# A Fourier layer and eight routed experts on one core: four transform chunks change their neighbours, and the experts' row and weight loads change their place in the load queue

## The chip, the core and the metric

The kernel runs on one core of a Trainium2 chip. The core has a matrix engine (TensorE, PE in the profile, with its weight loads shown apart as PEld), three engines for elementwise work (VectorE is DVE, ScalarE is ACT, GpSimd is POOL) and SyncE (SP), which here does nothing but issue DMAs. Each engine runs its own instructions in order and waits on semaphores for the others. The metric is the device time of one execution in microseconds (us); smaller is better.

## The reference, cut to what matters

```python
# x is (8, 2496, 256); all arrays are float32
X = np.fft.rfft(x, axis=1)
Yr = Xr @ w_r - Xi @ w_i + b_r          # 256 x 256, the same for every frequency
Yi = Xr @ w_i + Xi @ w_r + b_i
Yr, Yi = shrink(Yr, 0.01), shrink(Yi, 0.01)   # sign(v) * max(|v| - 0.01, 0)
y = np.fft.irfft(Yr + 1j * Yi, n=2496, axis=1)

t = y.reshape(19968, 256)
logits = t @ w_gate + modality_bias[modality_id]      # 8 experts
e = argmax(logits); gate = softmax(logits)[e]
out = gate * (relu(t @ w1[e]) @ w2[e])                # 256 -> 1024 -> 256
```

## The kernel before

The transform over 2496 points is split as 39 times 64, and float32 operands are split into a high and a low part of which three products are summed. The work of one batch row (called a batch here, `b` = 0 to 7) goes through four steps on TensorE, and two batches are always in work:

- **Chunks** (`s1_chunk`, lines 298 to 320): the first transform, over 39 points. A batch has 11 chunks, each three matmuls of 117 rows by 512 columns (L311, L312, L313) into one PSUM bank, which ACT copies out (L316). Every second chunk SP writes 480 KB to a scratch in DRAM (L320). Each chunk needs its input split first (`s1_split`: a cast at L293 and a subtraction at L295).
- **Mixing stage** (ten pairs `p`): the second transform (L372), the products with the weights (L391, L403) and the shrinking (L408, L409). The loads of it come back from the scratch (`a_load`, L360).
- **64-row transform** (`is2_group`, five groups `g`): the first step back. Its matmuls (L431) use 64 of TensorE's 128 rows each and run in pairs, one on the upper 64 rows and one on the lower. DVE and ACT copy the two banks of a group out (L435).
- **Transposing products** (22 steps `j`): `pivot` (L445) gives 128-row products that ACT casts (L450) and DVE subtracts (L451); `is1` (L457 to L459) does the last transform on them three products at a time. Between them stand two pairs of the next batch's mixing stage (`s2`, at the start and after j = 15).

The order on PE, ACT, DVE and POOL is written out by hand in `build`; SP's order is set by the framework's scheduler. The chunks of batch b + 2 are dealt out over batch b. For b = 1 to 5, five of the eleven stand in the mixing stage (c = 0 to 4), four in the 64-row transform behind its groups 0 to 3 (c = 5 to 8), two among the transposing products (c = 9 and 10, at j = 8 and 11). For batch 0, four stand in the 64-row transform and seven among the transposing products. For batches 6 and 7 there are none left.

Lines 1551 to 1555 are the place in the 64-row transform:

```python
for g in range(5):
    at.is2_group(b, g)
    ...
    if b + 2 < nb and g < 4:
        at.s1_chunk(*s1.pop(0), inverse=True)
        at.s1_split(b + 2, 7 + g if b else 4 + g)
```

Behind the eighth batch come the **experts** (`Experts.run`). Rows were scattered by expert to DRAM (`xs`), and 40 units `i` go over them: 38 of 512 rows and two of 256. A unit has two halves (`grp` 0 and 1); in each, the first layer's products of one half (L1048) and the second layer's of another (L1119) take turns on PE. Unit i + 2's rows come by `load_x` (four DMAs L915, and L917), and its weights in four parts by `load_w(i + 2, n)` (n = 0 and 1: L882 or L883 and L884; n = 2 and 3: L877), on SP's queue. From the ninth unit on a weight part is only fetched when the expert changes. `prep(i + 2)` transposes the rows on DVE (L934) in the second half of unit i. Five of the units also carry a small remainder tile (`tiny`), whose raw weights are loaded by `load_raw` (L893, L897). Before, the rows of unit i + 2 and weight part 0 are asked for at the start of unit i, parts 1 and 2 in its middle, part 3 at its end.

Of the kernel before, what the change touches and what calls it, by code (L numbers as in the profile page):

```python
# [45 lines left out]
EARLY = (6 * SEQ - 8 * (TP - 1)) // TP + 1 - E  # L46
# [771 lines left out]
class Experts:  # L818
# [438 lines left out]
    def run(self, late, *tail):  # L1257

        nc = self.nc
        U = NP + NS  # L1260
        self.tags = {NPL - 1: [2, 4, 5, 6]}
        for i in range(NPL - 2, -1, -1):
            t = self.tags[i + 1]
            self.tags[i] = [t[3]] + [j for j in range(7) if j not in t]
        pieces = self.weight_sums()
        for i in range(2):
            self.load_x(i)
        self.rt.grid2 = self.rt.load_grid(self.cp, "c_grid2", 5 * E + 3)
        for n in range(4):
            self.load_w(1, n)  # L1270
            if n == 0:
                next(pieces)
        self.fold = self.cp.tile([128, TINY], F32, name="fold")
        with self.tc.issue_after(tail[0].ins), self.tc.issue_after(tail[1].ins):
            for _ in chain(self.prep(0), self.sums(0), self.parts(0)):
                pass
        nc.vector.reduce_sum(self.fold, self.ident.rearrange("p (g t) -> p t g", t=TINY), AX.X)
        self.fill(5)
        for _ in self.layer1(0, 0):
            pass  # L1280
        for _ in self.prep(1):
            pass
        every = (U - 8) // SLOTS
        for i in range(U):
            if i + 2 < U:
                assert i + 2 < EARLY or self.rt.late
                if i == NPL - 2:
                    assert next(pieces, None) is None
                self.load_x(i + 2)
                self.load_w(i + 2, 0)  # L1290
            k, at = divmod(U - 2 - i, every)
            k = U + SLOTS - 1 - k
            small = U <= k < U + SLOTS
            if small and at == 2:
                self.load_x(k)
                self.stage = self.load_raw(k)
            if small and at == 1:
                self.sort_half(k)
            if small and at == 0:
                self.side = self.tiny(k)  # L1300
            for grp in range(2):
                one = self.layer1(i + grp, 1 - grp) if i + grp < U else iter(())
                n1 = (8 if i + grp < NPL else 7 if i + grp < NP else 4) if i + grp < U else 0
                n2 = 2 * self.subs(i)
                two = self.layer2(i, grp)
                fill = {"o": iter(()), "x": self.parts(i + 1) if grp == 0 and i + 1 < U else iter(()),
                        "t": self.sums(i + 1) if grp == 0 and i + 1 < U else iter(()),
                        "p": self.prep(i + 2) if grp == 1 and i + 2 < U else iter(())}
                if self.rest:
                    fill["o"], self.rest = self.last(*self.rest), None  # L1310
                fills = self.FILL[grp] if grp or i >= NPL else self.FILL2 if i == NPL - 1 else self.FILL1
                for n, c in enumerate(self.order(n1, n2)):
                    next(one if c == "1" else two)
                    for f in fills.get(n, ""):
                        next(fill[f], None)
                    if n in self.LATE:
                        next(late, None)
                    if i < NPL - 2:
                        next(pieces, None)
                    if c == "2":  # L1320
                        next(self.stage, None)
                        if n % 3 == 0:
                            next(self.side, None)
                for g in (one, two, fill["o"], fill["t"], fill["x"], fill["p"]):
                    for _ in g:
                        pass
                if i + 2 < U:
                    if grp == 0:
                        self.load_w(i + 2, 1)
                    self.load_w(i + 2, 2 + grp)  # L1330
        for _ in self.side:
            pass
        self.finish(*self.rest)

        k = U + SLOTS
        more = nc.values_load(self.rt.ti[k:k + 1, 3:4], min_val=0, max_val=1,
                              skip_runtime_bounds_check_because="a flag")
        with self.tc.If(more > 0):  # L1338
            for i in range(k, k + MORE):
                self.load_x(i)  # L1340
                for _ in self.load_raw(i):
                    pass
                self.sort_half(i)
                self.half(i)
# [37 lines left out]
def build(tc, I, out, nb):  # L1382
    nc = tc.nc
    with ExitStack() as outer:
# [3 lines left out]
        with ExitStack() as ctx:  # L1388
            at = Attn(tc, I, nb)
# [15 lines left out]
            def s2(i, split=None):  # L1405
                if i < last:
                    low.append(at.s2_pair(*divmod(i, 10), ld.pop(i)))
                    xs[i] = next(low[-1])
                if split:
                    at.s1_split(*split)  # L1410

            def s2_low():
                for g in low:
                    next(g)
                low.clear()
# [48 lines left out]
            s1 = [(1, c) for c in range(11)]  # L1464
            for b in range(nb):
                done = b == nb - 1
                for p in range(10):
                    i = 10 * b + p
# [43 lines left out]
                    if b and p == 5 and b + 2 < nb:  # L1512
                        s1 = [(b + 2, c) for c in range(11)]
# [30 lines left out]
                if b == 0:  # L1544
                    at.s1_load(2, 5)
                    s1 = [(2, c) for c in range(11)]
                for g in range(5):
                    at.is2_group(b, g)
                    if done:
                        rt.scatter(2, at.mark)  # L1550
                    if not done and g in (1, 3):
                        sw.step()
                    if b + 2 < nb and g < 4:
                        at.s1_chunk(*s1.pop(0), inverse=True)
                        at.s1_split(b + 2, 7 + g if b else 4 + g)
                s2(10 * b + 10)
                more = 8
# [2 lines left out]
                for j in range(J):  # L1560
                    pend.append((j, at.pivot(b, j)))
                    if (j + 1) * left // J != j * left // J:
                        rt.scatter(1, at.mark)
                    if j == 15:
                        s2(10 * b + 11)
                    if len(pend) > 2:
                        jj, r = pend.pop(0)
                        at.is1(b, jj, *r, nc.scalar.copy if done or jj % 2 else nc.vector.tensor_copy)
                    if j in (2, 17):
                        s2_low()  # L1570
                    if not done and j in ((14, 19) if b else (9, 14, 19)):
                        sw.step()
                    if j == 6:
                        rt.bias(b)
                    if j % 3 == 2 and (j > 6 or b == 0) and s1:
                        at.s1_chunk(*s1.pop(0), inverse=True)
                    if b == 0 and j % 3 == 2 and more < 11:
                        at.s1_split(2, more)
                        more += 1
                    next(routing, None)  # L1580
# [62 lines left out]
```

## Time and profile before

| what | us |
|---|---|
| median of 3 runs | 1467.63 (1466.71 to 1468.15) |
| the profiled execution's own time | 1459.45 |
| its span, from first to last instruction | 1457.7 |
| PE busy in the span | 1415.0 (97%) |
| PEld busy in the span | 1354.5 (93%) |
| DVE, ACT, POOL busy in the span | 892.4, 779.9, 791.7 (61%, 54%, 54%) |

The profile is of one execution. A group row gives the busy time of like instructions and the idle time of the engine before them; a window row gives every engine's busy time in a stretch, with the number of its instructions, the granted clock of TensorE (1.00 is 2.4 GHz, 0.50 is 1.2 GHz) and the share of the DMA engines' time. In a timeline a row is one instruction, or several alike, with its start, its duration, and in brackets the idle time before it and what ended that. A matmul's duration is longer than the distance to the next one, since they are pipelined: what a matmul costs is the distance between starts.

### The profile page before, as it was taken

To read this page: it belongs to the slowest core of one execution; us is meant where nothing else is said; L and a number is where in the kernel's file an instruction comes from. 1 tells how busy PE (TensorE), PEld (TensorE's weight loads), DVE (VectorE), ACT (ScalarE), POOL (GpSimd) and SP (SyncE) were. 2 spreads that over 40 slices of the span, in tenths; PEclk is the share of its full clock that TensorE was granted. 3 is DMA by queue.
4 is the path that set the end of the run, shared out by engine and by line. 5 is a ranking of instruction groups with operands and counts; after the bars stand their busy time and mean duration, and the time that the engine had idled before them with its cause. 6 is when DMAs were issued, how large, how long until landed. Compare 5 with 4: busy or idle time off the path is not lost. (4 is left out here: it accounts for less than half of the span.)

```text
span 1457.7 us, 33928 instructions
## 1 busy us (share of the span) xinstructions
PE 1415.0 (97%) x12122; PEld 1354.5 (93%) x12122; DVE 892.4 (61%) x1729; ACT 779.9 (54%) x1690; POOL 791.7 (54%) x905
## 2 busy tenths in 40 slices
PE   8999999999999998999999999999999999999996
PEld 7898989898989888999999999899999999999995
DVE  6666666565666675667764565566656656666651
ACT  5566565555555352644435555455555555555542
POOL 2547676766677565366657644344444444454442
PEclk9999999999999999999999999999999999999999
DMA  8779686968686658488779369214212962592192
GB/s 299 212 216 293 205 289 209 291 203 278 191 293 188 213 160 283 158 235 267 224 280 280 87 223 319 55 40 111 59 43 54 291 196 46 170 308 60 38 335 106
DMA packets 242240, 284.54 MB, mean 195 GB/s; under 512 B 120761, under 2 KB 173865, under 8 KB 238995
## 3 DMA queue, kind: packets, MB, share of 16 engines
q1 hardware_dynamic: 222769, 240.22, 53.8%
q0 software_dynamic: 19168, 42.04, 9.0%
q8 instruction: 98, 1.61, 0.5%
q14 instruction: 75, 0.61, 0.1%
q10 hardware_dynamic: 130, 0.06, 0.0%
HBM read 320.24 MB, written 114.86 MB: 298 GB/s over the span
## 5 line engine op out<-in xcount | busy, mean ns | idle before, releaser
L1119 PE MATMUL y<-w,hh 128*128 128x256 f32 x2496 | 455.9, 277 | 0.0
L1119 PEld LDWEIGHTS y<-w,hh 128*128 128x128 f32 x2496 | 377.7, 189 | 3.7 <-issue 3.7
L1119 PE MATMUL y<-w,hl 128*128 128x256 f32 x1248 | 346.1, 277 | 1.5 <-DVE hl L1054 1.4
L1048 PE MATMUL X<-xh,w 128*128 128x256 f32 x1248 | 265.6, 278 | 2.0 <-issue 2.0
L1152 POOL DMA_INDIRECT out<-o,ix x156 | 155.5, 997 | 174.1 <-ACT o L1136 139.6
L1119 PEld LDWEIGHTS y<-w,hl 128*128 128x128 f32 x1248 | 235.1, 188 | 2.3 <-DVE hl L1054 2.1
L1048 PEld LDWEIGHTS X<-xh,w 128*128 128x128 f32 x1248 | 212.1, 189 | 4.1 <-issue 2.2
L1048 PE MATMUL X<-xl,w 128*128 128x256 f32 x624 | 173.2, 278 | 0.6 <-POOL xl L983 0.6
L1054 DVE SCALAR_TENSOR_TENSOR hl<-Y,hh 128x512 fp32r<-128x512 f32 x140 | 96.8, 691 | 99.3 <-ACT hh L1053 80.2
L1053 ACT ACTIVATE hh<-Y 128x512 fp32r<-128x512 f32 x140 | 83.8, 599 | 113.5 <-DVE Y L1057 93.6
L983 POOL TENSOR_TENSOR xl<-tr,xh 128x256 fp32r<-128x256 f32 x94 | 70.6, 751 | 119.4 <-ACT xh L982 118.4
L1048 PE MATMUL Z<-xh,w 128*128 128x256 f32 x608 | 128.8, 277 | 3.2 <-DVE Y L1057 3.2
L983 POOL TENSOR_TENSOR xl<-xt,xh 128x256 fp32r<-128x256 f32 x122 | 88.7, 746 | 67.2 <-ACT xh L982 67.0
L403 PE MATMUL mx<-wmix,Xh 128*128 128x256 f32 x640 | 116.1, 304 | 7.6 <-DVE mx L393 3.4
L619 POOL DMA_INDIRECT xs<-x1b,si x88 | 90.1, 1024 | 53.6 <-DVE pl L451 22.2
L1048 PEld LDWEIGHTS X<-xl,w 128*128 128x128 f32 x624 | 117.8, 189 | 1.1 <-POOL xl L983 0.8
L1062 ACT COPY v<-X 128x512 f32<-128x512 f32 x180 | 105.6, 587 | 16.5 <-PE X L1048 11.6
L619 POOL DMA_INDIRECT xs<-x,si x88 | 88.8, 1009 | 40.6 <-issue 19.6
L445 PE MATMUL pv<-pv,z 128*120 128x136 f32 x704 | 108.8, 280 | 1.7 <-DVE pl L451 0.8
L1048 PEld LDWEIGHTS Z<-xh,w 128*128 128x128 f32 x608 | 102.8, 188 | 3.6 <-DVE Y L1057 3.6
L403 PEld LDWEIGHTS mx<-wmix,Xh 128*128 128x128 f32 x640 | 92.4, 190 | 14.8 <-issue 5.8
L451 DVE TENSOR_TENSOR pl<-pv,ph 120x264 fp32r<-120x264 f32 x176 | 74.7, 430 | 50.9 <-ACT ph L450 33.3
(265 smaller groups left out, 3437.3 us busy)
## 6 DMA issues: line engine op xcount, KB each, us to landing
w<-wsp SPq DMA_DIRECT2D x96, 1024.0 KB
w<-wss SPq DMA_DIRECT2D x64, 1024.0 KB
w<-wsp SPq DMA_DIRECT2D x64, 768.0 KB
xt<-xs SPq DMA_DIRECT2D x152, 128.0 KB
x<-in_x SPq DMA_DIRECT2D x35, 512.0 KB
a<-scr SPq DMA_DIRECT2D x140, 128.0 KB
scr<-ev SPq DMA_DIRECT2D x35, 480.0 KB
wsp<-wh SPq DMA_DIRECT2D x64, 256.0 KB
```

Source lines behind the costliest of these rows:

```text
L403: nc.tensor.matmul(mx[:, i, :], t[:, c, 1 - i, :], self.w[:, i, c, lo, :], start=False, stop=n == 5, skip_group_check=True)
L445: nc.tensor.matmul(ps[:PK, c * 128:c * 128 + D // 2 + E], self.z[:, o:o + 3, :, :].rearrange("p n k r -> p (n k r)"), self.pv[:, c, :], st ...
L451: self.mark = nc.vector.tensor_sub(pl, ps[:PK, :GC], ph)
L619: i = self.nc.gpsimd.indirect_dma_start(out=self.xs, out_offset=bass.IndirectOffsetOnAxis(ap=si[:, k:k + 1], axis=0), in_=rows, in_offset= ...
L983: (nc.gpsimd if i or j in (0, 1, 6) else nc.vector).tensor_sub(sq(xl), v, sq(xh))
L1048: nc.tensor.matmul(ps[:, u, :], w1[:, lo, u, blk, :], x, start=start and u == k == 0, stop=k == 2, skip_group_check=True)
L1053: nc.scalar.activation(hh[:, par::2, o], v, AF.Relu)
L1054: nc.vector.scalar_tensor_tensor(hl[:, par::2, o], v, 0.0, hh[:, par::2, o], ALU.max, ALU.subtract)
L1062: nc.scalar.copy(v, ps)
L1119: nc.tensor.matmul(ps, h[:, q, o], w2[:, lo, q, :], start=grp == s % 2 == q == k == 0, stop=grp == 1 and q == 3 and k == 2, skip_group_che ...
L1152: ins = self.nc.gpsimd.indirect_dma_start(out=self.out, out_offset=bass.IndirectOffsetOnAxis(ap=ix, axis=0), in_=o, in_offset=None, bounds ...
```

## The change

Three things change, and no instruction is added or taken away.

For batches 1 to 5 no chunk stands in the 64-row transform any more. The four go among the transposing products, where the chunks now stand at j = 5, 8, 11, 14, 17 and 20. The input of the last one is split behind j = 5 instead of behind group 3. Batch 0 stays as it was.

In the experts, rows are asked for half a unit sooner, in the middle of unit i for unit i + 3, where the rows are complete by then. Weight part 2 moves from the middle of the unit to slot 7 of its second half.

```diff
@@ Experts.run
             if i + 2 < U:
-                assert i + 2 < EARLY or self.rt.late
                 if i == NPL - 2:
                     assert next(pieces, None) is None
-                self.load_x(i + 2)
+                if i + 2 not in self.xt:
+                    assert i + 2 < EARLY or self.rt.late
+                    self.load_x(i + 2)
                 self.load_w(i + 2, 0)
...
+                    if grp and n == 7 and i + 2 < U:
+                        self.load_w(i + 2, 2)
...
+                if grp == 0 and i + 3 < U and (i + 3 < EARLY or self.rt.late):
+                    self.load_x(i + 3)
                 if i + 2 < U:
-                    if grp == 0:
-                        self.load_w(i + 2, 1)
-                    self.load_w(i + 2, 2 + grp)
+                    self.load_w(i + 2, 3 if grp else 1)
@@ build, 64-row transform
-                    if b + 2 < nb and g < 4:
+                    if b == 0 and g < 4:
                         at.s1_chunk(*s1.pop(0), inverse=True)
+                    if b + 2 < nb and g < 4 and (g < 3 or b == 0):
                         at.s1_split(b + 2, 7 + g if b else 4 + g)
@@ build, transposing products
-                    if j % 3 == 2 and (j > 6 or b == 0) and s1:
+                    if j % 3 == 2 and (j > 3 or b == 0) and s1:
                         at.s1_chunk(*s1.pop(0), inverse=True)
+                        if b and j == 5:
+                            at.s1_split(b + 2, 10)
```

On PE, between groups 0 and 1 of batch 1's 64-row transform (`zs_0`, `zs_1` are the groups' banks, `s_3_5` is chunk 5 of batch 3):

```order
 L431 MATMUL zs_0_z<-c_q,x_67 128x128
 L431 MATMUL zs_0_x<-c_q,x_67 128x128
-L311 MATMUL s_3_5_1825<-x1h_5_1732,c_f 120x512
-L312 MATMUL s_3_5_1825<-x1h_5_1732,c_f 120x512
-L313 MATMUL s_3_5_1825<-x1l_5_1733,c_f 120x512
 L431 MATMUL zs_1_z<-c_q,x_67 128x128
 L431 MATMUL zs_1_x<-c_q,x_67 128x128
```

The chunk is gone from there, and group 1 follows group 0; the same holds behind groups 1 to 3, and in batches 2 to 5.

On PE, among batch 1's transposing products, where that chunk now stands (`pv_5` and `pv_6` are steps 5 and 6, `i_1_3` is the last transform of step 3):

```order
L445 MATMUL pv_5_2001<-pv,z_1804 120x136 x2
L457 MATMUL i_1_3_2011<-ph_3_1977,c_g 117x264
L458 MATMUL i_1_3_2011<-ph_3_1977,c_g 117x264
L459 MATMUL i_1_3_2011<-pl_3_1978,c_g 117x264
L311 MATMUL s_3_5_2016<-x1h_5_1732,c_f 120x512
L312 MATMUL s_3_5_2016<-x1h_5_1732,c_f 120x512
L313 MATMUL s_3_5_2016<-x1l_5_1733,c_f 120x512
L445 MATMUL pv_6_2026<-pv,z_1804 120x136 x2
```

Before, step 6 followed directly on the last transform of step 3.

On SP, behind the first loads of a remainder tile's raw weights (`x_67<-in_moe_w`), where `w_0_7707` is weight part 1, `w_0_7703` and `w_0_7704` are parts 2 and 3, and `xt` and `g` are unit 15's rows; before:

```order
L897 DMA x_67<-in_moe_w 128x2x256
...
L883 DMA w_0_7707<-wsp 128x4x384
...
L884 DMA w_0_7707<-wss 128x4x512
...
L877 DMA w_0_7703<-wsp 128x2048
...
L877 DMA w_0_7704<-wsp 128x2048
...
L915 DMA xt_12668<-xs 32x16x64
...
L917 DMA g_12669<-xs 128x4x2
```

and now:

```order
L897 DMA x_67<-in_moe_w 128x2x256
...
L915 DMA xt_12538<-xs 32x16x64
...
L917 DMA g_12539<-xs 128x4x2
...
L883 DMA w_0_7707<-wsp 128x4x384
...
L884 DMA w_0_7707<-wss 128x4x512
...
L877 DMA w_0_7703<-wsp 128x2048
...
L877 DMA w_0_7704<-wsp 128x2048
```

The rows' loads stood behind the three remaining weight parts and stand ahead of them now.

## Rows read from the trace of the kernel before

**Rows 1.** The page, busy time of each engine over the span:

```profile
PE 1415.0 (97%) x12122; PEld 1354.5 (93%) x12122; DVE 892.4 (61%) x1729; ACT 779.9 (54%) x1690; POOL 791.7 (54%) x905
```

**Rows 2.** Windows, the 64-row transform of batches 1 to 7, one row each:

```profile
core 0: us, PE busy (x) PEld busy (x) DVE busy (x) ACT busy (x) POOL busy (x), PEclk, DMA share, GB/s
...
133.15:147.42 14.27, 14.12 (x173) 11.55 (x172) 4.06 (x6) 7.55 (x13) 10.29 (x11) 1.00 0.72 220
206.49:220.35 13.86, 13.64 (x173) 11.18 (x172) 4.07 (x6) 7.66 (x13) 10.91 (x11) 1.00 0.65 194
277.65:292.75 15.10, 14.31 (x173) 11.62 (x172) 4.15 (x6) 7.43 (x13) 12.03 (x13) 1.00 0.74 238
350.33:368.24 17.91, 15.93 (x174) 12.98 (x173) 4.07 (x6) 7.70 (x13) 11.63 (x12) 0.90 0.63 196
426.76:441.45 14.69, 14.45 (x173) 11.67 (x172) 4.15 (x6) 7.36 (x13) 12.39 (x13) 1.00 0.71 223
499.85:509.88 10.03, 10.03 (x161) 9.91 (x160) 4.00 (x10) 3.33 (x5) 6.69 (x7) 0.90 0.49 165
567.37:583.90 16.53, 13.37 (x162) 11.76 (x161) 4.65 (x7) 4.16 (x7) 9.19 (x10) 0.90 0.91 249
```

**Rows 3.** Timeline of PE (start us, duration us, line, operands), batch 2's 64-row transform:

```profile
214.61 0.49 PE L311 MATMUL s<-x1h,c_f 117*120 117x512 f32 x1
...
215.50 0.37 PE L431 MATMUL zs_z<-c_q,x1b 64*128 64x128 f32 x1
...
215.72 0.27 PE L431 MATMUL zs_z<-c_q,x1b 64*128 64x128 f32 x1
...
217.28 0.27 PE L431 MATMUL zs_z<-c_q,x1b 64*128 64x128 f32 x1
...
217.49 0.49 PE L311 MATMUL s<-x1h,c_f 117*120 117x512 f32 x1
```

**Rows 4.** Timeline of PE, a chunk among batch 2's transposing products:

```profile
228.69 0.40 PE L311 MATMUL s<-x1h,c_f 117*120 117x512 f32 x1
...
229.39 0.63 PE L445 MATMUL pv<-pv,z 128*120 128x136 f32 x4
```

**Rows 5.** Timeline of PE, step 16 and the next mixing stage, batches 0 and 1:

```profile
91.99 0.63 PE L445 MATMUL pv<-pv,z 128*120 128x136 f32 x4
...
99.98 0.27 PE L372 MATMUL s<-c_m,a 128*128 128x128 f32 x1
...
163.88 0.63 PE L445 MATMUL pv<-pv,z 128*120 128x136 f32 x4
...
171.92 0.27 PE L372 MATMUL s<-c_m,a 128*128 128x128 f32 x1
```

**Rows 6.** Groups of ACT (count, busy us, mean ns, idle), same 64-row transform:

```profile
L435 ACT COPY z<-zs_x 128x512 f32<-128x512 f32 x4 | 2.7, 669 | 4.9 <-PE s L313 2.7 <-PE zs_x L431 2.3
L293 ACT CAST x1h<-x 117x512 fp32r<-117x512 f32 x4 | 2.5, 624 | 0.0
```

**Rows 7.** Windows, expert units 12, 13 and 15, then a stretch from 914.80:

```profile
872.49:892.89 20.40, 20.40 (x182) 20.40 (x181) 13.00 (x20) 11.69 (x26) 9.76 (x14) 1.00 0.98 318
892.89:917.51 24.62, 21.97 (x182) 21.77 (x181) 13.16 (x21) 11.75 (x26) 9.28 (x12) 0.94 0.79 252
...
942.41:962.81 20.40, 20.40 (x182) 20.40 (x181) 13.02 (x20) 11.69 (x26) 9.25 (x12) 1.00 0.26 53
...
914.80:918.20 3.40, 3.40 (x19) 3.40 (x18) 2.46 (x4) 1.32 (x3) 0.00 (x0) 0.50 0.01 2
```

**Rows 8.** Timeline of SP, then DVE and PE, unit 13's loads and wait:

```profile
887.54 5.22 SPq L897 DMA_DIRECT2D x<-in_moe_w  x4
...
897.05 8.86 SPq L915 DMA_DIRECT2D xt<-xs  x4
...
912.12 1.31 DVE L934 STREAM_TRANSPOSE tr<-xt 128x512 f32<-128x512 f32 x2 [5.35 <-DMA xt<-xs]
...
914.07 0.39 PE L1048 MATMUL Z<-xh,w 128*128 128x256 f32 x1 [2.65 <-DVE Y L1057]
```

## The prediction, made before the changed kernel was run

> **What bounds the kernel now.** I read the page's busy times first. PE is busy 97% of the span [rows 1], no other engine over 61%, so the end moves only when PE's own time moves. The change adds and removes no PE work. It can pay only where the same matmuls take longer in one place than in another, or where PE waits. So I read the windows by step next, and then PE's timeline inside them, by the distance between starts.
>
> The 64-row transforms are the first such place [rows 2]. Batches 1 to 5, each with four chunks, take 14.27, 13.86, 15.10, 17.91 and 14.69 us, together 75.83. Batch 6, with none, takes 10.03, and by the row's mean clock of 0.90 some 2 us of that lie at half the clock. Batch 7, with none either, takes 16.53. The reader is to see two things: what four chunks cost there, and that this step stumbles in some batches for a reason that isn't the chunks alone.
>
> The Trainium skill ("Trainium Kernel Development and Optimization", Best Practices) says to judge a kernel's distance to its limit by the weight loads' busy share and not by the matmuls'. Here the two differ: in batch 2's transform matmuls leave 0.22 us of 13.86 idle and weight loads 2.68 [rows 2]. By the first the step has nothing to give, by the second some 2.7 us a batch. The sum below is made from neither, but from distances between starts, and comes out nearer to the second.
>
> The experts are the second place. A unit takes 20.40 us with PE and PEld busy throughout (units 12 and 15), which is its floor; unit 13 takes 24.62 [rows 7].
>
> **The chunks, in their old place.** In batch 2, from one chunk's first matmul (214.61) to the next one's (217.49) there are 2.88 us, for one chunk and one group [rows 3]. A group is 16 pairs; from the second pair (215.72) to the last (217.28) there are 14 steps in 1.56 us, 0.111 each, so a group by itself is 16 x 0.111 = 1.78. The chunk costs 2.88 - 1.78 = 1.10. There are 4 x 5 = 20 of them: **-22.0 us**. Five groups without chunks would take 8.9, with four chunks 13.3; batches 1 to 5 stand 1.0, 0.6, 1.8, 4.6 and 1.4 above that, 9.3 in all. The trace names no engine for most of it, so the forecast keeps it at 9.3. Its bounds are 0 and what batch 7 shows, below.
>
> **In their new place.** Among the transposing products a chunk takes 229.39 - 228.69 = 0.70 [rows 4], since neighbours and chunk use the rows alike; where a chunk stands between two 64-row pairs, the first start after either change of rows comes late: 217.49 is 0.21 after the last pair where pairs are 0.11 apart, and the pair at 215.72 is 0.22 behind the one at 215.50 [rows 3]. Four more in five batches are at most 20 x 0.70 = +14.0. But some of that is covered. From step 16 to the next mixing stage, batch 1 without a chunk takes 171.92 - 163.88 = 8.04 us, and batch 0 with two chunks in the same stretch takes 99.98 - 91.99 = 7.99 [rows 5]. There the chunks fill the gaps in which PE waits for the copies of the products, so the two at j = 17 and 20 are nearly free. I charge 0.70 each for j = 5 and 14 and 0.1 for the other two together: 1.5 a batch, **+7.5**. The bounds are 5 x 1.4 = 7.0 and 14.0; I stay near the lower, since batch 0 is the same code with the same chunks at the same steps.
>
> **What else moves with them.** ACT's copy of a chunk and the scratch write behind it go along. The four copies leave a step where ACT is busy 7.66 of 13.86 us [rows 2] and go to one with the same copies in batch 0. SP writes the last scratch part nine steps later, at the end of the batch; it is read in the second half of the next mixing stage, which for batch 1 lasts from 171.92 [rows 5] to 206.49 [rows 2], so over 15 us on, and I cost that at nothing. If that cover went, s2 of the batch after next would wait. The split of chunk 10 waits for chunk 5's matmuls on ACT, whose copy out stands ahead of it in ACT's queue and waits for the same matmuls: nothing is added.
>
> **The experts' loads.** In unit 13 SP issues the raw weights from 887.54, three weight parts, and only at 897.05 the rows of unit 15, whose four DMAs take 8.86 us to issue alone. DVE's transposes wait 5.35 us for them, until 912.12, and in DVE's queue the additions of the running unit stand behind: PE waits 2.65 [rows 8]. The clock follows: after that wait the granted clock is 0.50, 1.2 GHz, from 914.80 to 918.20 [rows 7], which costs up to half of 3.4, and unit 13 stands 24.62 - 20.40 = 4.22 over its floor. With the change these rows stand directly behind the raw weights and ahead of the weight parts, more than 12 us earlier and well before the transposes want them. **-4.2**. In the other units the rows are in time already (units 12 and 15 have no idle PE), so asking sooner gives nothing there. The loads now wait until POOL has finished with the buffer's rows, and weight part 1 queues behind them on SP; it and part 2 are wanted over a unit later, 20.40 us, so a few us of delay are covered. I cost it at 0, between 0 and one more wait like unit 13's, +4.2.
>
> **Sum.** -22.0 + 7.5 - 4.2 = **-18.7 us** against the profiled execution's 1459.45 (its span is 1457.7): 1440.8. The median of the runs shown, 1467.63, is 8.2 above the profiled execution; I carry that over unchanged: 1467.63 - 18.7 = **1449**.
>
> **The rivals.**
>
> *The 64-row transform stumbles when it runs bare (slower).* For it speaks batch 7: no chunk, 16.53 us, PE idle for 3.2 of it, half the clock in part. If the five steps all took that, 5 x 16.53 - 75.83 = +6.8, and the sum is +6.8 + 7.5 - 4.2 = +10.1, or 1477.7. The change loses from the point where the five average over (75.83 - 7.5 + 4.2) / 5 = 14.5 us. Against it: batch 6 ran bare without a gap, and batch 7's DMA share is 0.91 against 0.63 to 0.74 in batches 1 to 5 [rows 2], since the experts' first loads run there. The copies out are no reason for it: ACT has 0.67 of copy and 0.62 of cast per group [rows 6], 1.29 in 1.78. The Trainium skill ("TensorEngine Tiling (Array Packing)", PSUM Bottleneck) warns that packing speeds up TensorE but not the copies out of PSUM, which may then be the bound. By that rule the bare step would be bound by the copies; by the rows ACT fits with 0.49 to spare. Chance 0.09.
>
> *The opposite: the stumbling goes as well,* because the step is over sooner. All 9.3 go too: 1439.6. Batch 6 speaks for it. Chance 0.18.
>
> *No cover.* All four chunks cost their 0.70, -22.0 + 14.0 - 4.2 = -12.2, or 1455.4. It would show as step 16 to the mixing stage at 9.4 instead of 8.0. Against it stands batch 0. Chance 0.15.
>
> *The experts give nothing:* the wait moves to another load or another unit. -14.5, or 1453.1. For it: the DMA share is 0.98 in unit 12 [rows 7], so something comes late there anyway. Chance 0.13.
>
> *No difference,* with new waits in the experts of the size of the gain, 3 or 4 of 4.2 each: 1465 to 1467. Chance 0.05.
>
> The forecast itself has the remaining 0.40. That the change doesn't do what it says is excluded by the order: the chunks and the rows stand where they should.
>
> **How the numbers follow.** The likeliest time is 1449. A run of this kernel can tell about 0.2%, 3 us, from no change, so faster means under 1464.7. The forecast, no cover, the experts' rival and the opposite are all faster, 0.86 together; I take 0.02 off for two of the small ones meeting. Faster 0.84, same 0.07, slower 0.09. For the range, the lower end is the opposite's 1439.6 less some 2.6 for unit waits that may go with the earlier rows: 1437. The upper end is the no-cover and experts rivals together (-8.0, 1459.6) with one more wait of 3.4: 1463. Left out are the slower rival, no difference, and little of the rest.
>
> **What would show it.** Right: the 64-row transforms of batches 1 to 5 at 9 to 11 us; the transposing products of these batches 1.4 to 2 us longer; unit 13 at 20.4, its transposes ended by nothing; one stretch less at half clock. Wrong: a 64-row transform over 14.5 us, idle "issue" gaps between its pairs; a transpose waiting for its rows in another unit; the first matmuls of a mixing stage waiting for pairs loaded from the scratch.

## The result, and the profile after

The kernel after takes 1456.85 us (median of 9 runs), the kernel before 1467.63 (9 runs): a ratio of 0.9918, 95% interval 0.9894 to 0.9941, so 9 to 16 us less. One of the nine runs after took 1730.04 us at a mean granted clock of 0.76 and is left out of the ratio. The prediction said 1449 in 1437 to 1463.

The two profiled executions don't show it: 1459.78 after and 1459.45 before. That of before was shorter than any of its nine timed runs (1463.65 to 1474.36). So the stages have to be compared one by one. The page of the kernel after has the same busy share of PE as [rows 1]:

```profile
span 1458.0 us, 33914 instructions
...
PE 1410.8 (97%) x12122; PEld 1359.0 (93%) x12122; DVE 894.5 (61%) x1729; ACT 777.4 (53%) x1690; POOL 792.3 (54%) x905
```

Windows of the kernel after, the 64-row transforms of batches 1, 2, 4 and 7 (columns as in [rows 2]):

```profile
134.65:146.41 11.76, 10.58 (x161) 9.61 (x160) 4.06 (x6) 4.71 (x8) 8.97 (x10) 1.00 0.48 156
207.70:220.82 13.12, 11.72 (x162) 10.96 (x161) 4.06 (x6) 4.71 (x8) 8.67 (x10) 0.87 0.48 168
...
354.20:365.30 11.10, 10.28 (x161) 9.66 (x160) 4.06 (x6) 4.81 (x8) 9.63 (x10) 1.00 0.55 181
...
564.24:585.51 21.27, 14.03 (x162) 12.53 (x161) 4.66 (x7) 4.46 (x7) 12.12 (x14) 0.84 0.94 288
```

Batches 1 to 5 take 58.8 us together, where [rows 2] have 75.8: 17.0 less. They still stumble: the sum is some 13 above five bare steps, which take 9.13 each where nothing stumbles (below). Batch 7, which the change leaves alone, took 21.27 where [rows 2] have 16.53; these 4.7 are one reason why the two executions are equally long. The transposing products of batches 1 to 5 went from 116.7 to 129.0, 12.3 more, where the forecast had 7.5. PE's timeline of the kernel after shows one reason, from step 16 of batch 1 to the next mixing stage:

```profile
164.52 0.63 PE L445 MATMUL pv<-pv,z 128*120 128x136 f32 x4
...
165.99 0.72 PE L445 MATMUL pv<-pv,z 128*120 128x136 f32 x4 [0.47 <-DVE pl L451]
...
173.36 0.83 PE L372 MATMUL s<-c_m,a 128*128 128x128 f32 x6
```

These are 8.84 us, where [rows 5] have 8.04 without the chunks and 7.99 in batch 0 with them. The experts' windows, units 12 and 13 of the kernel after:

```profile
875.83:897.03 21.20, 21.20 (x183) 21.20 (x181) 13.02 (x20) 11.76 (x26) 9.71 (x14) 1.00 1.07 379
897.03:918.23 21.20, 21.20 (x183) 21.20 (x181) 13.04 (x20) 11.75 (x26) 9.31 (x12) 1.00 0.87 254
```

Unit 13 has lost its wait and its half clock [rows 7, 8]: 21.20 for 24.62. But units 10 to 13 stand at 21.20, where [rows 7] have 20.40 in unit 12, although PE never idles and the granted clock is 1.00. Their matmuls stand 118 ns apart instead of 113.

### The profile page after: what moved, and what is told of

It is laid out like the page before. It is cut to its first block, busy times and chain, and to the rows that moved or that the text cites. A ratio compares the mean times of both kernels' runs of the same rounds, so it can differ in the third digit from the quotient of the medians.

```text
span 1458.0 us, 33914 instructions
## 1 busy us (share of the span) xinstructions
PE 1410.8 (97%) x12122; PEld 1359.0 (93%) x12122; DVE 894.5 (61%) x1729; ACT 777.4 (53%) x1690; POOL 792.3 (54%) x905
## 5 line engine op out<-in xcount | busy, mean ns | idle before, releaser
L983 POOL TENSOR_TENSOR xl<-tr,xh 128x256 fp32r<-128x256 f32 x94 | 70.6, 751 | 120.4 <-ACT xh L982 119.7
L1048 PE MATMUL Z<-xh,w 128*128 128x256 f32 x608 | 129.0, 278 | 0.6 <-issue 0.6
L983 POOL TENSOR_TENSOR xl<-xt,xh 128x256 fp32r<-128x256 f32 x122 | 88.7, 747 | 65.8 <-ACT xh L982 65.6
L445 PE MATMUL pv<-pv,z 128*120 128x136 f32 x704 | 110.5, 283 | 5.4 <-ACT z L435 3.0
L445 PEld LDWEIGHTS pv<-pv,z 128*120 128x120 f32 x704 | 96.6, 185 | 11.5 <-DVE pl L451 4.5
```

What stands on the lines that cost most here:

```text
L445: nc.tensor.matmul(ps[:PK, c * 128:c * 128 + D // 2 + E], self.z[:, o:o + 3, :, :].rearrange("p n k r -> p (n k r)"), self.pv[:, c, :], st ...
L983: (nc.gpsimd if i or j in (0, 1, 6) else nc.vector).tensor_sub(sq(xl), v, sq(xh))
L1048: nc.tensor.matmul(ps[:, u, :], w1[:, lo, u, blk, :], x, start=start and u == k == 0, stop=k == 2, skip_group_check=True)
```

## The experiments

There were twelve runs, on three chips. The kernel before ran beside them each time, and each ratio is to its runs on the same chip: 1433.22 us for chunks_only, experts_only, chunks_row and scatter_into, 1431.41 for before_again, after_again and split_later, 1465.82 for chunks_only_2, experts_only_2, after_2 and split_scatter and 1459.74 for even_scatter, both on the third chip. On the first two chips nothing stumbles as it does in both profiles above; they are called undisturbed here, and they settled most points.

**chunks_only and experts_only.** The change taken apart: one has only the diff's hunks in `build`, the other only those in `Experts.run`.

```diff
@@ chunks_only (kernel before plus)
-                    if b + 2 < nb and g < 4:
+                    if b == 0 and g < 4:
                         at.s1_chunk(*s1.pop(0), inverse=True)
...
-                    if j % 3 == 2 and (j > 6 or b == 0) and s1:
+                    if j % 3 == 2 and (j > 3 or b == 0) and s1:
...
@@ experts_only (kernel before plus)
...
+                if grp == 0 and i + 3 < U and (i + 3 < EARLY or self.rt.late):
+                    self.load_x(i + 3)
...
```

> Only the chunks are moved; the experts' loads stand as before. Theory (both parts pay where the sum says): by the two profiles the 64-row transforms of batches 1 to 5 give 17.0 and their transposing products take back 12.3, so this should come out 4 to 6 us under the kernel before, with unit 13 at about 24.6 and its transposes waiting for the rows again. Rival (the chunks carry nearly all of the measured 11 us, and the profiled execution after happened to stumble more than most): 8 to 11 us under before. Second rival (the chunks give nothing net): within 2 us of before.

> Only the experts' loads are moved; the chunks stand as before. Theory: unit 13 loses its wait for the rows, 3.4 us by the profile after, and unit 9 some more, so 3 to 5 us under before. Rival (what unit 13 wins, units 10 to 13 give back by the wider spacing of their matmuls, 118 ns instead of 113, that the profile after shows): within 2 us of before, with units 10 to 13 at 21.2 each. Second rival (this part carries most of the 11 us): 7 us or more under before.

chunks_only: 1422.32, ratio 0.9924 (0.9907 to 0.9941), 10.9 us less. experts_only: 1433.61, ratio 1.0004 (0.9988 to 1.0021), nothing. Both went to a rival: on this chip the chunks carry the gain. In experts_only's profile unit 13 has no wait, and units 9 to 13 stand at 21.20 each, as that rival said; units 8 to 13 sum to 126.6. In chunks_only's profile they sum to 127.5 at the same pace, and unit 13, with the old loads, hardly waits:

```profile
838.99:860.19 21.20, 21.20 (x183) 21.20 (x181) 13.02 (x20) 11.78 (x26) 9.70 (x14) 1.00 1.00 322
860.19:881.69 21.50, 21.41 (x183) 21.21 (x181) 12.49 (x20) 11.17 (x25) 9.29 (x12) 1.00 0.83 261
```

Here, at the slower pace, the rows come nearly in time without being asked for sooner.

**chunks_row.** Is it the change of rows that a chunk costs between groups? The four chunks stand in a row behind the last group.

```diff
-                    if b + 2 < nb and g < 4:
+                    if b == 0 and g < 4:
                         at.s1_chunk(*s1.pop(0), inverse=True)
+                    if b + 2 < nb and g < 4 and (g < 3 or b == 0):
                         at.s1_split(b + 2, 7 + g if b else 4 + g)
+                if b and b + 2 < nb:
+                    for n in range(4):
+                        at.s1_chunk(*s1.pop(0), inverse=True)
+                        if n == 0:
+                            at.s1_split(b + 2, 10)
```

> The kernel before, with the four chunks of batches 1 to 5 behind the last group of the 64-row transform instead of between its groups: the matmuls stay in the same stretch and only the changes between 64 and 128 rows fall from eight to two a batch. Theory (a chunk between groups costs 1.10 because of the changes of rows, 0.70 among its like): 20 x 0.40 = 8 us less in the stretch from the first group to the first transposing product, a batch at 8.9 + 2.8 = 11.7 plus its stumbling, and the time 5 to 8 us under before. Rival (the changes of rows cost nothing, a chunk there costs its 1.10 for another reason, or the stumbling comes whatever the order): within 2 us of before, the stretch as long as before.

1428.55, ratio 0.9957 (0.9939 to 0.9975): 4.7 us less by the medians, 6.2 by the ratio, about the theory's lower end. Windows of batch 3, the transform, then the four chunks with one more group of the next mixing stage up to the first transposing product:

```profile
275.99:285.12 9.13, 9.13 (x162) 9.01 (x161) 4.06 (x6) 4.81 (x8) 8.13 (x8) 1.00 0.59 188
285.12:289.45 4.33, 4.29 (x23) 3.02 (x21) 0.70 (x1) 3.44 (x6) 3.32 (x4) 1.00 0.57 179
```

Together 13.46, against 14.46 for the same stretch in before_again, below: 1.00 a batch saved of the 1.6 that the theory had. A chunk in a row costs 0.84, and the excess over 0.70 is not a change of rows. The row brings no change of its own, since the transform ends in one in any case; all eight between the groups are gone. PE's weight loads show what the third and the fourth chunk wait for, ACT's copies of the first and the second, and so it is in all five batches:

```profile
286.76 0.18 PEld L311 LDWEIGHTS s<-x1h,c_f 117*120 117x120 f32 x1 [0.42 <-ACT ev L316]
...
287.76 0.18 PEld L311 LDWEIGHTS s<-x1h,c_f 117*120 117x120 f32 x1 [0.48 <-ACT ev L316]
```

```profile
286.12 0.59 ACT L316 COPY ev<-s 120x512 f32<-120x512 f32 x1 [0.18 <-PE s L313]
286.60 0.62 ACT L293 CAST x1h<-x 117x512 fp32r<-117x512 f32 x1
287.12 0.59 ACT L316 COPY ev<-s 120x512 f32<-120x512 f32 x1
```

The two chunks start 0.15 and 0.20 late, and their second matmul follows 0.10 later than elsewhere: 0.55 a batch, which is all of the excess.

**before_again and after_again.** Both kernels as they are, for their profiles on one undisturbed chip.

> The kernel before, unchanged, for its profile beside the others of this call. The first four experiments ran where the kernel before took 1433.22 us, 34 less than in the runs behind the prediction, and their profiles show no 64-row transform that stumbles: every one with chunks takes 13.46 or 13.47 us there and every one without 9.13 or 9.14. Theory (the stumbling belongs to the chip that a run meets, not to the program): the profile here shows 13.47 in all of batches 1 to 5 if the time is near 1433, and 14 to 18 with stretches at half the clock if it is near 1468. Rival (the stumbling belongs to this program's order, and chunks_row, experts_only and chunks_only lack it because their order is another): over 14 in some of the batches although the time is near 1433.

> The kernel after, unchanged. chunks_only came out 0.9924 of before [0.9907 to 0.9941] and experts_only 1.0004 [0.9988 to 1.0021]. Theory (the gain is the chunks', and a unit of the experts wins nothing on balance): 0.990 to 0.994, transposing products at 25.1 in batches 1 to 5, 64-row transforms at 9.13, and units 8 to 13 at 21.2 instead of 20.4 wherever PE's matmuls stand 118 ns apart. Rival (the two parts help each other): under 0.988.

before_again took 1432.35, 1.0007 of before (0.9989 to 1.0025); after_again 1416.15, 0.991 (0.9888 to 0.9932), 13 us less by the ratio. The first theory held, and of the second the ratio and the stages; but after_again has units 8 to 13 at 20.40, the faster pace, so that the experts do win something here. Windows of batch 2 in before_again, the 64-row transform and the transposing products:

```profile
208.51:221.97 13.46, 13.46 (x173) 11.18 (x172) 4.17 (x6) 7.80 (x13) 10.41 (x11) 1.00 0.70 209
...
222.97:245.15 22.18, 22.16 (x174) 21.23 (x173) 15.17 (x39) 14.46 (x39) 15.79 (x18) 1.00 0.65 192
```

and in after_again:

```profile
203.97:213.11 9.14, 9.14 (x162) 9.02 (x161) 4.13 (x6) 4.82 (x9) 7.53 (x9) 1.00 0.58 203
...
214.10:239.20 25.10, 25.08 (x187) 23.43 (x186) 15.43 (x39) 16.81 (x44) 21.32 (x24) 1.00 0.77 235
```

All five batches read alike to 0.02 us. There is no stumbling, with the same program: it needs something that the program doesn't set. Whether that is the chip itself or something else about a set of runs isn't shown; the third chip stumbled in both of its sets. From step 16 of batch 1 to the mixing stage, first before_again, then after_again:

```profile
166.30 0.63 PE L445 MATMUL pv<-pv,z 128*120 128x136 f32 x4
...
173.03 0.72 PE L372 MATMUL s<-c_m,a 128*128 128x128 f32 x5
```

```profile
162.59 0.63 PE L445 MATMUL pv<-pv,z 128*120 128x136 f32 x4
...
170.56 0.61 PE L372 MATMUL s<-c_m,a 128*128 128x128 f32 x4
```

6.73 without chunks and 7.97 with them.

**split_later.** One step of the transposing products, from 8 to 9, takes 1.79 in after_again and 1.53 in the others with a chunk. Is it the split of chunk 10, which the change puts behind step 5?

```diff
-                        if b and j == 5:
-                            at.s1_split(b + 2, 10)
+                    if b and b + 2 < nb and j == 6:
+                        at.s1_split(b + 2, 10)
```

> The kernel after with one statement moved: the split of chunk 10 stands behind step 6 of the transposing products and not behind chunk 5's copy at step 5. Theory (the cast of that split stands in ACT's queue ahead of the cast of product 6, and the last transform of step 6 waits 0.26 for it): the step from 8 to 9 goes from 1.79 to 1.53 in batches 1 to 5 and the stage from 25.1 to 24.8, 1.3 us in all, too little to tell in the time. Rival (the 0.26 comes from the first use of the bank or from DVE, which makes the bias there): the step stays at 1.79.

The step went to 1.53 in all five batches and the stage from 25.09 to 24.82; 1415.66, ratio 0.9903 (0.9879 to 0.9927). The queue that it stood in, ACT's and then PE's rows of batch 1 in chunks_only:

```profile
150.05 0.59 ACT L316 COPY ev<-s 120x512 f32<-120x512 f32 x1 [0.33 <-PE s L313]
150.53 0.62 ACT L293 CAST x1h<-x 117x512 fp32r<-117x512 f32 x1
151.05 0.68 ACT L450 CAST ph<-pv 120x264 fp32r<-120x264 f32 x2
151.72 0.38 ACT L460 COPY x<-i 117x264 f32<-117x264 f32 x1
```

```profile
151.52 0.63 PE L445 MATMUL pv<-pv,z 128*120 128x136 f32 x4
152.15 0.38 PE L457 MATMUL i<-ph,c_g 120*117 120x264 f32 x1
```

```profile
152.15 0.18 PEld L457 LDWEIGHTS i<-ph,c_g 120*117 120x117 f32 x1 [0.21 <-ACT x L460]
```

L457 follows L445 by 0.38 elsewhere, and here by 0.63. The split's cast is the reason, but not by way of the cast of product 6, as the theory had it: that one has ended by 151.44, and what releases L457 is ACT's copy L460, which stands behind both casts and ends at 152.10.

**chunks_only_2, experts_only_2, after_2.** The same kernels once more, on the third chip, which stumbles as the first profiles do.

> chunks_only once more, beside the kernel after and experts_only. Theory (the chunks give 10 us, the loads 0 to 4 according to the pace that PE's matmuls fall into in units 8 to 13): 0.992 to 0.994 of before; in its profile either unit 13 waits for its rows, about 4 us, with units 8 to 12 at 20.40, or units 8 to 12 stand at 21.20 and unit 13 hardly waits, so that units 8 to 13 sum to 126 to 128 either way. Rival (the loads give their 4.2 in every execution): units 8 to 13 differ from those of the kernel after by 4 whatever the pace.

> experts_only once more. Theory (the gain hangs on the pace): 0.997 to 1.001 of before; where its profile shows units 8 to 13 at 20.40 throughout, they sum to 122.4, 4 less than with the wait, and where it shows 21.20 they sum to 126 to 127 and nothing is won. Rival (the loads win 4.2 and the first experiment missed it by chance): 0.996 to 0.998 and no unit over 21.

> The kernel after once more, on the same chip as chunks_only_2. Theory: 0.990 to 0.993 of before, 0 to 3 us under chunks_only_2. Rival (the loads give their 4.2 in full): 4 us or more under chunks_only_2.

1463.56, ratio 0.9982 (0.9964 to 1.0); 1463.66, ratio 0.9981 (0.9963 to 1.0); 1458.05, ratio 0.9957 (0.9934 to 0.998). Here each half is worth 2 to 3 us, with intervals that reach to nothing, and both together 6 by the ratio and 8 by the medians. The expectation for chunks_only_2 missed: with the chunks moved the 64-row transforms of batches 1 to 5 sum to 62.4 there, against 80.3 in experts_only_2 and 45.7 undisturbed, so the stumbling takes back part of the gain. That for after_2 missed too. after_2 was 5.5 under chunks_only_2, which speaks for the rival that the loads give all of theirs on this chip, though by the ratios it is 3.7 and the intervals overlap. Units 10 to 13 sum to 81.9 in after_2 and to 85.8 in chunks_only_2, where unit 13 waits again (24.56). experts_only_2's time fits its theory and its rival alike; its profile has units 10 to 13 at 21.20. In all five profiles of this chip unit 9 takes 21.4 to 25.9, with old loads and with new; DVE's transposes wait there for POOL's subtraction L983, up to 3.2 us, and not for the rows.

**scatter_into, split_scatter, even_scatter.** What makes the 64-row transform stumble? In the first two profiles PE's gaps ("issue") fell in times when POOL's scatters were draining. These three deal the scatters of batches 1 to 5 out anew and leave PE's order alone. Of 22 a batch the kernel after has 11 in the mixing stage, none in the 64-row transform and 11 among the transposing products; scatter_into has 5, 10, 7, split_scatter 6, 5, 11, and even_scatter 8, 3, 11. The last two also have split_later's edit.

```diff
@@ split_scatter
-                    if p > 3:
+                    if p > 3 and not (0 < b < 6 and p > 4):
                         rt.scatter(1, at.mark)
...
-                    if done:
-                        rt.scatter(2, at.mark)
+                    if done or 0 < b < 6:
+                        rt.scatter(2 if done else 1, at.mark)
@@ even_scatter: p > 6 for p > 4, and behind groups 0, 2 and 4 alone
```

> The kernel after, with POOL's scatters of the routed rows dealt out otherwise in batches 1 to 5: 5 instead of 11 in the mixing stage, 10 behind the groups of the 64-row transform (none before), 7 instead of 11 among the transposing products. PE's own order is untouched. Theory (PE stumbles, and its signals come late, while the scatters' queue drains): the five 64-row transforms rise from 58.8 us together to 65 or more, and the transposing products lose part of their wait at step 16 (1.46 us for that step, 0.83 in batch 0, which has no scatters). Rival (the stumbling comes from the 64-row matmuls themselves or from all DMA together): the 64-row transforms stay between 54 and 62 and step 16 at 1.4 to 1.5.

> split_later, with POOL's second scatter of a pair left out from pair 5 on in batches 1 to 5 and one scatter behind each group of the 64-row transform instead; among the transposing products nothing changes. Theory (in the last pairs of the mixing stage DVE's subtraction of a split takes 1.5 to 2.5 us instead of 0.69 while POOL, late by its scatters, subtracts another one, and PE waits for DVE): the time from the last pair's first product to the 64-row transform, 4.54 to 6.3 in these batches, is 4.5 to 5.1, 2 to 4 us less in all than in split_later, and the transposing products stay at 24.8. Rival (the scatters are not the reason): 4.5 to 6.3 as before, or the same waits in the 64-row transform instead, which would then be over 9.13.

> split_later with POOL's scatters dealt out more evenly than in split_scatter: in batches 1 to 5 eight in the mixing stage (the second one of a pair left out from pair 7 on), one behind groups 0, 2 and 4 of the 64-row transform, eleven among the transposing products as in the kernel after. PE's own order is untouched. split_scatter took all stumbling out of the 64-row transforms (9.13 in all five), but its transposing products rose to 27.7 to 28.6, where the last five scatters now met the next eleven. Theory (PE stumbles where scatters stand in a row on POOL without other work between them, on chips where it stumbles at all): where the kernel before takes about 1465, the five 64-row transforms stay under 10 each and the transposing products under 26, and the time is 0.985 to 0.990 of before; where before takes about 1432, 9.13 and 24.8 as in split_later, and 0.988 to 0.992. Rival (each scatter costs PE its share wherever it stands): where before takes about 1465, the two stages together stay near the 37.3 us a batch of split_scatter, and the time at 0.991 to 0.993.

scatter_into ran on the first, undisturbed chip: 1423.26, ratio 0.9922 (0.9895 to 0.9949), every 64-row transform at 9.13, though POOL starts four scatters in a row within each of them. The five sum to 45.7, under both sides of the expectation. So scatters alone don't do it, and the run tells nothing about a chip that stumbles. The other two ran on the third chip: split_scatter 1451.23, ratio 0.9912 (0.9889 to 0.9934), and even_scatter 1446.03, ratio 0.9906 (0.9887 to 0.9924). Windows of batch 2, the transform and the transposing products, in after_2, split_scatter and even_scatter:

```profile
207.43:218.52 11.09, 10.39 (x161) 9.58 (x160) 4.06 (x6) 4.82 (x8) 9.62 (x10) 1.00 0.54 181
219.52:244.90 25.38, 25.36 (x186) 23.48 (x185) 15.37 (x39) 16.78 (x44) 18.18 (x20) 1.00 0.71 206
```

```profile
205.77:214.90 9.13, 9.13 (x162) 9.01 (x161) 4.06 (x6) 4.81 (x8) 5.13 (x6) 1.00 0.56 191
215.89:244.44 28.55, 26.65 (x186) 24.99 (x185) 15.27 (x39) 16.81 (x44) 23.99 (x26) 0.94 0.70 211
```

```profile
206.02:215.82 9.80, 9.65 (x161) 9.34 (x161) 4.06 (x6) 4.72 (x9) 7.50 (x8) 1.00 0.60 212
216.99:243.07 26.08, 25.14 (x184) 23.47 (x185) 15.27 (x39) 16.73 (x44) 21.17 (x24) 1.00 0.68 211
```

POOL starts three scatters in a row within each transform in after_2, the rest of those queued in the mixing stage, and in split_scatter two, 1.8 to 2.3 us apart. There all five transforms take 9.13, while those of batches 6 and 7, whose scatters stand as before, take 11.87 and 20.49 in the same execution: on a chip that stumbles, the stumbling left the five with the scatters. Against the expectation it came back among the transposing products, 140.6 for five against 127.5 in after_2, where POOL now runs late and its scatters stand close. even_scatter has 46.6 and 131.9; both stages together are 35.7 a batch, against 37.2 in split_scatter, 36.8 in after_2 and 34.0 in split_later undisturbed. That is nearer to the theory than to the rival, though the products stayed over its 26. By time the two can't be told apart, and even_scatter's ratio lies between both expectations. The other part of split_scatter's theory, 4.5 to 5.1 from the last pair's first product to the transform, held but for one batch: 4.57, 5.46, 4.56, 4.55, 4.69, against 4.67 to 6.08 in after_2. So split_scatter beats the kernel after on the same chip, 0.9912 against 0.9957, with intervals that just meet; its gain beside split_later on an undisturbed chip wasn't measured.

## Why the prediction was right, and where it was not

**A chunk between groups costs 1.10: right.** Undisturbed, four chunks go and the step falls from 13.46 to 9.14: 1.08 each, 21.7 in all for a forecast of 22.0. The bare five groups take 9.13, for 8.9. That the changes of rows are the reason, chunks_row shows: the eight of a batch make 4 x (1.08 - 0.70) = 1.5, of which it gets 1.0 back, and the rest it loses to waits for ACT's copies. Of the two figures weighed there, the weight loads' idle time (2.7 a batch) and the matmuls' (0.2), neither came near 4.3. And the copies out of PSUM did not bind: the bare step shows no wait at 9.13, as the row on ACT's 1.29 in 1.78 had it. On the chips that stumble the step gave less, 18.8 on average, since there the bare steps stand 13.6 above their undisturbed 45.7 and those with chunks 10.7 above their 67.3.

**Two of the four are covered: wrong.** This is the step that failed. It took 8.04 us from step 16 to the mixing stage in [rows 5] for the normal state, and read its gaps as cover. Undisturbed the stretch is 6.73 without a chunk and 7.97 with two: batch 0's figure, 7.99, was right for the kernel after, and the 1.3 above 6.73 were stumbling, which batch 0, without scatters, never had. So undisturbed all four chunks pay, 2 x 0.70 at j = 5 and 14 and 1.24 at j = 17 and 20. On chips that stumble the gaps are there and cover part of the last two: averaged over batches 1 to 5 the stretch takes 7.9 and 8.0 with the chunks in their old place (before, experts_only_2) and 8.4 to 8.7 with the chunks in it (after, chunks_only_2, after_2), some 0.6 more, where 0.1 was charged. The sign stood in the same profile: batch 0's steps took 0.83 without a chunk at places where batch 1's took up to 1.30.

**The split adds nothing: wrong, 1.3 us.** The prediction looked at what the split waits for, and not at what stands behind it. Two casts and the copy L460 do, in ACT's queue, and split_later takes the 0.26 a batch away. With it the products cost 5 x 2.91 = 14.5 more undisturbed, for 7.5: 13.2 by the chunks, near the no-cover rival's 14.0, and 1.3 by this.

**Nothing else moves: wrong, both ways.** Undisturbed, the mixing stages are shorter by 2 to 8 us in all, 5.5 on average: the seven from batch 1 on take 230 to 232 in the four kernels with the chunks moved to the transposing products, and 235 to 237 in the three without. Some 2.4 of it is the third pair of batches 2 to 6, 3.16 instead of 3.58 to 3.70 (scatter_into, whose scatters are dealt out otherwise, keeps the longer one and gains elsewhere). POOL finishes its subtraction before DVE's first routing step and no longer stands beside it. Batch 3 in before_again, DVE's row and POOL's:

```profile
249.01 1.36 DVE L555 TENSOR_TENSOR L<-x1b,b 117x176 f32<-117x176 f32 x1
```

```profile
248.89 1.29 POOL L1374 TENSOR_TENSOR wl<-wr,wh 128x512 fp32r<-128x512 f32 x1
```

In after_again DVE's row takes 0.33. On chunks_only's own chip the mixing stages are 2.2 and 5.0 shorter than in the two kernels without; the chunks' sum is then -21.7 + 14.5 and -2 to -5, that is -9 to -12, and chunks_only measured -10.9. On the chips that stumble the third pair is 3.16 in the old place too (in before and experts_only_2), and there the stages are longer with the chunks moved: 236 to 238 (after, chunks_only_2, after_2) against 234 and 235.

**Unit 13's wait is worth 4.2: right where the pace holds.** before_again has 24.41 there, after_again 20.40, units 8 to 13 sum to 126.4 and 122.4. But next to nothing of it shows where PE falls into the pace of 118 ns, 0.8 us a unit; experts_only gave 0 and experts_only_2 3 us (0 to 5). Over all profiles units 10 to 13 average 85.8 with the old loads (five, 85.1 to 86.7) and 83.4 with the new (nine: 81.6 to 81.9 in four and 84.8 to 84.9 in five, at the slower pace). The term was mis-sized, at 2.4 on average and 0 to 5 between two profiles. The slower pace shows there in five of nine profiles with the new loads and in one of five with the old; whether the loads have a part in it isn't shown. The reading behind the term was a little off as well: in the profile after, unit 15's rows are asked for 4.0 us ahead of unit 13's start, where [rows 8] have them 4.2 behind [rows 7], so 8.2 sooner and not over 12. It was enough.

**The stumbling stays: right in kind.** 9.3 was carried over; the profile after shows 13, after_2 11. The rival in which it goes is out on such a chip, and so is the one in which the bare step is as bad as batch 7: the largest mean over batches 1 to 5 is 12.5, in chunks_only_2, under the 14.5 from which it decides. Of the prediction's own signs, the transforms came to 11.1 to 13.1 in the profile after, not to 9 to 11, and the "issue" gaps between pairs, named as a sign of being wrong, are there.

**The size.** The time came out 8 above the forecast, within its range. Undisturbed, the cover and the split are 7.0 of what the sum had wrong, and the mixing stages gave 5.5 that it didn't have. On chips that stumble, with the chunks moved (after, chunks_only_2, after_2) against not moved (before, experts_only_2), the transforms of batches 1 to 5 give 18.8 of 22.0, the products take 11.1 for 7.5, and the mixing stages take 2.6 for nothing; with 2.2 from units 10 to 13 that is some 7 us less in all, between the 12 (9 to 16) of the result and the 6 (3 to 10) of after_2. The time is near that of the no-cover rival, 1455.4. Its mechanism holds undisturbed, if not by its sign: it named 9.4 for step 16 to the mixing stage, where 8.0 over a base of 6.7 is the same loss. On a chip like that of the result part of the cover stands and other terms make up for it, so that its number fits is in part luck.

## What to carry to other kernels

A gap beside a place in the trace may belong to a disturbance and not to the program: look for the same place without it, in another batch of the same profile, before counting on the gap as cover. When a statement moves, list what stands behind it in each in-order queue, and price a move between stages by the steady distance between starts in both. Profile before and after more than once, since two single profiles here had the same length for kernels that differ by 11 us.

## What the runs showed of the hardware

**PE can stop while POOL's scatters go out, on some chips.** In after_2's 64-row transform of batch 2, PE's rows, with nothing that it waits for, and POOL's beside them:

```profile
211.65 0.35 PE L431 MATMUL zs_x<-c_q,x1b 64*128 64x128 f32 x1 [0.15 <-issue]
...
212.38 0.37 PE L431 MATMUL zs_x<-c_q,x1b 64*128 64x128 f32 x1 [0.20 <-issue]
213.10 0.36 PE L431 MATMUL zs_x<-c_q,x1b 64*128 64x128 f32 x1 [0.35 <-issue]
```

```profile
208.67 0.99 POOL L619 DMA_INDIRECT xs<-x,si  x1 [0.30 <-issue]
209.97 0.98 POOL L619 DMA_INDIRECT xs<-x,si  x1 [0.30 <-issue]
211.26 0.99 POOL L619 DMA_INDIRECT xs<-x,si  x1 [0.31 <-issue]
212.25 0.62 POOL L1376 CAST wh<-wr 128x512 fp32r<-128x512 f32 x1
```

after_again has five such scatters in a row in the same transform, the last at 209.93, and not one gap. What differs between the chips, or between the sets of runs on them, no run tells; that the scatters' places decide where PE stumbles, split_scatter does.

**PE has two paces at one granted clock.** The experts' matmuls stand 113 or 118 ns apart, 20.40 or 21.20 us a unit, at clock 1.00 and with no idle time. At the changes that were traced closely there is a break: a wait (chunks_only at 698, 1.3 us), a start 0.1 us late (experts_only at 779), or the remainder tile in unit 14, behind which unit 15 takes 20.40 in every profile. Which pace a break leaves, no run foretells: the same wait in chunks_row, 1.7 us at 706, left 113.

**DVE stands still while POOL works on.** In chunks_only, batch 4's mixing stage, a subtraction that takes 0.69 elsewhere, POOL's beside it, and what PE waited:

```profile
337.79 2.46 DVE L295 TENSOR_TENSOR x1l<-x,x1h 117x512 fp32r<-117x512 f32 x1
```

```profile
337.38 0.99 POOL L619 DMA_INDIRECT xs<-x,si  x1 [0.30 <-issue]
338.40 1.29 POOL L295 TENSOR_TENSOR x1l<-x,x1h 117x512 fp32r<-117x512 f32 x1
```

```profile
341.00 0.71 PE L403 MATMUL mx<-wmix,Xh 128*128 128x256 f32 x4 [1.64 <-DVE mx L393]
```

DVE's ends 0.56 after POOL's. The Trainium skill ("SBUF — State Buffer", SBUF: two separate sides) says that a DVE operation with two inputs in SBUF and one of GpSimd that reads SBUF exclude each other for a whole instruction, and that the one that starts first goes first. The rows agree with the first part: nearly all of DVE's 0.69 fits behind POOL's end. They don't show the second: by its record DVE's starts 0.61 before POOL's and still ends after it, with a scatter on POOL just ahead, and no run tells whether that had a part.
